# Placing the second batch's key maxima and value sums on VectorE: behind the weight conversions instead of among them

## The chip, the cores and the metric

One core of a Trainium2 chip runs the whole program. The metric is the device time of one execution in microseconds. TensorE (PE) does the matrix products, VectorE (DVE), ScalarE (ACT) and GpSimd (POOL) the work around them, SyncE (SP) starts the transfers. The order of the instructions on each engine's queue is fixed when the program is built.

## The reference, cut to what matters

Three layers follow each other on 2 x 768 tokens of width 512; the weights arrive as 8-byte floats.

```
k_sum = k.reshape(B, H, nb, 32, D).max(axis=3)      # 24 blocks of 32 keys: maximum of each
v_sum = v.reshape(B, H, nb, 32, D).mean(axis=3)     # and the mean of each block's values
scores = [q k^T / 8 inside a window of 15 on each side | q k_sum^T / 8 + log 32]
x = softmax(scores) @ [v | v_sum]                   # 8 heads, 2 batches
xk, xr = token mixes of x with the token before
y = sigmoid(xr w_r) * (relu(xk w_k)^2 w_v)          # "first layer": w_k 512x1024, w_v 1024x512
u = y + token mixing (w_tok1, w_tok2);  out = u + relu(u w_ch1) w_ch2
```

The change touches only when `k_sum` and `v_sum` of the second batch are computed on DVE.

## The kernel before, in words

**Weights.** The matmuls of the layers take each float32 operand as two parts, a rounded high part and a remainder; three products make one. A weight arrives as 128 x 512 eight-byte numbers and goes through `Weights.step` (L142 to L170): ACT scales the upper words (L153), DVE shifts the lower words (L157), DVE joins both to a float32 tile `wf` (L163), ACT rounds it to the high part (L174), POOL subtracts for the low part (L175, called from `rounded`, L172). `wf` has two buffers (WF = 2), so the shift of weight n + 2 needs the subtraction of weight n done. The first layer has 16 such weights: `wk[0], wv[0], wk[1], ... wv[7]`, in this order (L244 to L247).

**Attention.** Batch 0 runs as 12 steps of one half of the heads and one tile of 128 tokens, batch 1 as 6 steps of a whole tile. A step is: score matmuls (`sp`, L367), the masked and negated scores with their row extremes on DVE (L385), the exponential on ACT (L387), for batch 1 a normalization on DVE and POOL (`n_stage`, L394), transposes on PE (`pt`, L405), and the products with the values (`pv`, L425). Each key tile `kw` carries 24 columns of block maxima on either side; they are written there by POOL (`kw_sums`, L293) from the tile `ks`, which DVE's maxima fill (`k_max`, L287: one instruction for each of the six key tiles). All score matmuls of a batch thus need all six maxima of that batch. The value means: DVE sums (`vt_sum`, L309, two instructions into `vrs`), PE transposes (`v_gather`, L318), ACT scales into `vs` (L320), and SP copies `vs` into each value tile (L339) ahead of the value products.

**First layer.** `main` (L590) goes through six chunks of 256 tokens. For a chunk, `mixed` (L523) makes the mixed input (POOL L533, DVE L534, ACT L535, DVE L536). Then four groups: matmuls `ko` with two `wk` weights (24 instructions, one PSUM buffer), `k2_tile` (ACT relu L556, DVE square L557, ACT L558, POOL L559), and `values`, which adds the products with two `wv` weights into `acc` (12 instructions). Group 3 of the first chunk needs the 13th and 15th weight for `ko`, the 14th and 16th for `acc`. Chunks 0 to 2 need only batch 0; chunk 3 needs the first two tiles of batch 1.

**What sets the order.** The loop at L674 writes attention and first layer alternately by estimated costs; that order is each instruction's priority, which `ahead(n)` raises (k2_tile by 300, the transposes and value products by 400). A planner then simulates the engines and puts on each engine's queue what is ready, by priority. Before the first batch-1 score step, `prep(1)` (L512) writes the six `k_max`, the two `vt_sum`, `kw_sums` and `v_gather`. Walking through the two generators with their costs, all 16 weight conversions of the first layer have been written before the first `k_max` of batch 1, but the planner is free to place the maxima and the sums wherever DVE is free and their data has arrived. `behind(inst, marks)` (L227) is a pure ordering in a queue: `inst` is placed after the marked instruction, without a semaphore. Batch 0's `vt_sum` already has such a mark (`lows`).

Of the kernel before, what the change touches and what calls it, by code (L numbers as in the profile page):

```python
# [14 lines left out]
ALU = mybir.AluOpType  # L15
AX = mybir.AxisListType
# [41 lines left out]
def fused_kernel(ctx, tc, q, k, v, vt, mu, w_k, w_v, w_r, w_t1, w_t2, w_c1, w_c2, out):  # L58
    nc = tc.nc
# [40 lines left out]
    class Slot:  # L100


        def __init__(self, pl, tag):
            self.pl, self.tag = pl, tag
# [16 lines left out]
    class Weights:  # L121


        def __init__(self):
            self.todo, self.loaded, self.rounded, self.pin, self.ahead = [], [], [], 0, AHEAD
            self.early = True

        def add(self, slot, src, use):
            self.todo.append((slot, src, use))
# [12 lines left out]
        def step(self):  # L142
            while len(self.loaded) < self.ahead and self.todo:
                self.load()
            if not self.loaded:
                return False
            slot, st, use = self.loaded.pop(0)
            fold = isinstance(use, Fold)
            wf = use.part() if fold else stage.tile([128, 512], F32, tag="wf", bufs=WF, name="wf")
            words = st.bitcast(I32).rearrange("p (n two) -> p n two", two=2)  # L150
            top = words[:, :, 1]

            a = nc.scalar.activation(top.bitcast(F32), top.bitcast(F32), AF.Prelu, scale=2.0 ** -112, alpha=2.0 ** 32)  # L153
            after(a)
            behind(a, self.rounded[-2:-1])
            wi = wf.bitcast(I32)
            d = nc.vector.tensor_scalar(wi, words[:, :, 0], 29, None, ALU.logical_shift_right)  # L157
            after(d)
            if self.pin & 1:
                tc.keep_in_program_order(a)  # L160
            if self.pin & 2:
                tc.keep_in_program_order(d)
            nc.vector.scalar_tensor_tensor(wi, top, 3, wi, ALU.logical_shift_left, ALU.bitwise_or)  # L163
            if fold:
                use.close(slot)
            else:
                pair = slot.split("w")
                self.rounded.append(rounded(pair, wf, nc.gpsimd))
                use(pair)
            return True  # L170

    def rounded(pair, src, eng):  # L172
        hi, lo = pair
        r = nc.scalar.copy(hi, src)  # L174
        eng.tensor_tensor(lo, src, hi.bitcast(F32), ALU.subtract)  # L175
        return r
# [50 lines left out]
    def behind(inst, marks):  # L227

        for m in marks:
            tc.add_manual_dep(inst.ins, m.ins.name,  # L230
                              mybir.DependencyInfo(mybir.DependencyClass.NoSync, mybir.DependencyReason.DATA), reason="queue order")

    def after(inst):

        behind(inst, mark[-1:])

    weights = Weights()
# [17 lines left out]
    def ahead(n):  # L255

        def wrap(fn):
            def run(*args, **kw):
                with tc.high_priority(n) if n else ExitStack():
                    return fn(*args, **kw)  # L260
            return run
        return wrap

    state = {}
    lows = []
# [16 lines left out]
    def k_max(b, t):  # L282

        st = state[b]
        keys = st["kw"][t][:, :, K0 + PAD:K0 + PAD + 128].rearrange("p a (n w) -> p a n w", w=BLOCK)
        n = 128 // BLOCK
        nc.vector.tensor_reduce(st["ks"][:, :, n * t:n * t + n], keys, AX.X, ALU.max)  # L287

    @ahead(HK)
    def kw_sums(b, t):  # L290
# [13 lines left out]
    @ahead(HR)  # L304
    def vt_sum(b, j):
        st = state[b]
        if j == 0:
            st["vr"] = at.tile([128, NP, NB], F32, tag="vrs", bufs=1, name="vrs")
        r = nc.vector.tensor_reduce(st["vr"][:, 2 * j:2 * j + 2], st.pop(("vt", j)), AX.X, ALU.add)  # L309
        if b == 0:  # L310
            behind(r, lows[-1:])

    @ahead(HR)
    def v_gather(b):
# [134 lines left out]
    def attention():  # L449
# [3 lines left out]
        for i in range(len(steps) + 1):  # L453
            if i < len(steps):
                b, t, es = steps[i]
                if b and t == 0:
                    yield from prep(b)
                zs = s_stage(b, t, es)
                if len(es) == 1:
                    for what, z, lag in zip((t_stage, v_stage), (zs[0], zs), LAGS):  # L460
                        slots.setdefault(min(i + lag, n0), []).append(((i + lag, lag), what, z))
                else:
                    slots[i + 1] = [((i, 1), n_stage, z) for z in zs] + [((i, 2), t_stage, z) for z in zs] + [((i, 3), v_stage, zs)]
                if i < SPIN_UNITS:
                    spin(SPIN)
                yield 0.95 * len(es)
                if es[-1] == 1 and t + 1 < NT:
                    kw_sums(b, t + 1)
                if b and t == 0:
                    vw_sums(b, 0)  # L470
                if i in VSUM:
                    vt_sum(0, VSUM.index(i))
                if i == VSUM[1]:
                    v_gather(0)
                    vw_sums(0, 0)
# [36 lines left out]
    def prep(b):  # L512

        for t in range(NT):
            k_max(b, t)
            yield HOLD / (NT + 2)
        for j in range(2):
            vt_sum(b, j)
            yield HOLD / (NT + 2)
        kw_sums(b, 0)  # L520
        v_gather(b)
# [124 lines left out]
    for kind in range(3):  # L646
        mc = at.tile([128, NC], F32, name=f"mask{kind}")
        mm = work.tile([128, 2, 128], F32, tag="t32", bufs=2, name="mm")
        for half in range(2):
# [3 lines left out]
            keys = m[:, NB:NC] if half == 0 else m[:, 0:NK]  # L653
# [10 lines left out]
    for t in range(NT):  # L664
        ahead(HK)(k_max)(0, t)
# [477 lines left out]
```

## Time and profile before

| | |
|---|---|
| time, median of 3 runs | 502.85 us (502.44 to 504.47) |
| span of the profiled execution | 502.8 us, 8800 instructions |
| PE busy | 487.9 us, 97% of the span |
| DVE busy | 316.6 us, 63% |
| ACT busy | 250.9 us, 50% |
| POOL busy | 217.4 us, 43% |
| chain that ended last | PE 75%, DMA 10%, DVE 8%, POOL 2%, ACT 2% |
| granted PE clock, mean | 0.990 |

The profiled execution took 502.8 us from its first to its last instruction, 0.05 us from the median of the runs. In the page's second part the span is cut into 40 slices of 12.6 us; the PE line reads 9 nearly throughout, with 7 in slices 5 and 7 (counted from 1), the DVE line reads 9, 8, 9, 9 and 8 in slices 3 to 7 (25 to 88 us), and the clock line falls to 8 in slices 7 and 8. Busy PE is not PE at full speed: a matmul record that waits or runs at a lower clock is only longer.

### The profile page before, as it was taken

How to read it: one execution, taken by the hardware profiler on the slowest of the kernel's cores; microseconds unless marked ns; L12 is line 12 of the kernel's file. 1: busy time of each engine (PE TensorE's matmuls, PEld its weight loads, DVE VectorE, ACT ScalarE, POOL GpSimd, SP SyncE). 2: the span in 40 equal slices, each digit the busy share in tenths (PEclk: the TensorE clock that was granted, in tenths of full speed). 3: DMA queues.
4: the chain of work that ended last, by engine and by line, in shares of the span. 5: the costliest groups of instructions: out<-in, count | busy, mean ns of one | idle time of the engine just before them, and what ended most of it. 6: DMA issues, size and time to landing. Idle time of an engine off the chain costs nothing.

```text
span 502.8 us, 8800 instructions
## 1 busy us (share of the span) xinstructions
PE 487.9 (97%) x3278; PEld 407.1 (81%) x3278; DVE 316.6 (63%) x638; ACT 250.9 (50%) x569; POOL 217.4 (43%) x266
## 2 busy tenths in 40 slices
PE   7999997999999999999999998999999999999996
PEld 3567785888888888888888887878898999989995
DVE  2888998641514355598889789646579638354352
ACT  1778746862544555686585455454554435111110
POOL 6335587862441447345516434774942813000000
PEclk9899998899999999999999999999999999999999
DMA  8999930221000650000551998639351405253102
GB/s 264 323 309 361 335 87 14 88 80 40 20 1 2 224 196 0 1 0 14 161 163 21 400 394 313 211 112 316 117 168 42 142 31 164 52 200 117 52 1 83
DMA packets 35914, 70.63 MB, mean 140 GB/s; under 512 B 3072, under 2 KB 12288, under 8 KB 35872
## 3 DMA queue, kind: packets, MB, share of 16 engines
q1 hardware_dynamic: 34288, 69.09, 42.0%
q10 hardware_dynamic: 1584, 0.98, 0.7%
q8 instruction: 26, 0.43, 0.3%
q14 instruction: 16, 0.13, 0.1%
HBM read 60.04 MB, written 9.44 MB: 138 GB/s over the span
## 4 chain that ended last, share of the span: by engine, by line
PE 75%; DMA 10%; DVE 8%; POOL 2%; ACT 2%; issue 1%; SPq 1%; DVEq 0%; POOLq 0%
PE ko L544 13%; PE acc L544 13%; PE o L955 12%; PE m L544 11%; PE o L983 7%; PE ro L544 7%; PE go L544 5%; DMA wst<-in_moe_w_k_dram 3%; DMA xT<-in_q_dram 3%; DMA ybuf<-in_v_dram 2%; DVE wf L163 2%; PE pv L425 2%; PE sp L367 2%; PE h L544 2%; DMA wst<-in_moe_w_ch_dram 1%
## 5 line engine op out<-in xcount | busy, mean ns | idle before, releaser
L175 POOL TENSOR_TENSOR w<-wf,w 128x512 fp32r<-128x512 f32 x50 | 69.1, 1387 | 77.3 <-ACT w L174 72.4
L544 PE MATMUL ko<-xh,w 128*128 128x256 f32 x384 | 76.3, 288 | 1.7 <-POOL w L175 0.9
L544 PE MATMUL m<-u,w 128*128 128x256 f32 x504 | 65.1, 283 | 0.8 <-DVE mw L846 0.7
L544 PEld LDWEIGHTS m<-u,w 128*128 128x128 f32 x504 | 63.4, 191 | 2.9 <-DVE mw L846 0.9
L544 PEld LDWEIGHTS ko<-xh,w 128*128 128x128 f32 x384 | 61.1, 188 | 5.4 <-POOL w L175 1.1
L544 PE MATMUL acc<-w,kh 128*128 128x512 f32 x192 | 61.7, 404 | 0.0
L955 PE MATMUL o<-w,gh 128*128 128x512 f32 x192 | 59.1, 391 | 0.0
L544 PE MATMUL ko<-xl,w 128*128 128x256 f32 x192 | 54.4, 283 | 1.1 <-DVE xl L536 1.1
L559 POOL TENSOR_TENSOR kl<-rl,kh 128x512 fp32r<-128x512 f32 x24 | 33.7, 1405 | 44.6 <-ACT kh L558 36.4
L163 DVE SCALAR_TENSOR_TENSOR wf<-wst,wf 128x512 int32<-128x512 int32 x50 | 47.6, 956 | 8.2 <-ACT wst L153 7.1
L174 ACT CAST w<-wf 128x512 fp32r<-128x512 f32 x50 | 30.9, 620 | 42.8 <-DVE wf L163 40.9
L557 DVE TENSOR_TENSOR rl<-rl 128x512 f32<-128x512 f32 x24 | 19.6, 819 | 48.4 <-ACT rl L556 48.2
L387 ACT ACTIVATE pe<-pe,mn 128x120 f32<-128x120 f32 x96 | 36.6, 383 | 14.6 <-DVE mn L385 14.3
L153 ACT ACTIVATE wst<-wst 128x512 f32<-128x512 f32 x62 | 41.1, 675 | 2.1 <-DMA wst<-in_moe_w_ch_dram 2.1
L544 PEld LDWEIGHTS acc<-w,kh 128*128 128x128 f32 x192 | 35.3, 192 | 7.3 <-ACT pe L387 0.3
L955 PEld LDWEIGHTS o<-w,gh 128*128 128x128 f32 x192 | 34.7, 188 | 6.2
L534 DVE SCALAR_TENSOR_TENSOR xk<-xT,mus,tmp 128x256 f32<-128x256 f32 x52 | 36.5, 733 | 4.1 <-POOL tmp L533 3.2
L544 PEld LDWEIGHTS ko<-xl,w 128*128 128x128 f32 x192 | 36.2, 188 | 2.1 <-DVE xl L536 1.3
L544 PE MATMUL acc<-w,kl 128*128 128x512 f32 x96 | 37.7, 403 | 0.0
L955 PE MATMUL o<-w,gl 128*128 128x512 f32 x96 | 37.1, 391 | 0.0
L544 PE MATMUL go<-u,w 128*128 128x512 f32 x144 | 35.6, 393 | 0.0
L784 ACT ACTIVATE gh<-m 128x512 fp32r<-128x512 f32 x24 | 14.2, 596 | 42.7 <-DVE m L846 42.7
(120 smaller groups left out, 964.5 us busy)
## 6 DMA issues: line engine op xcount, KB each, us to landing
wst<-in_moe_w_ch_dram SPq DMA_DIRECT2D x36, 512.0 KB, 6.9
w<-stored SPq DMA_DIRECT2D x24, 512.0 KB, 4.9
stored<-w SPq DMA_DIRECT2D x24, 256.0 KB, 4.7
wst<-in_moe_w_k_dram SPq DMA_DIRECT2D x8, 512.0 KB, 7.4
wst<-in_moe_w_v_dram SPq DMA_DIRECT2D x8, 512.0 KB, 9.5
wst<-in_moe_w_tok_dram SPq DMA_DIRECT2D x6, 512.0 KB, 4.7
out_dram<-o SPq DMA_DIRECT2D x12, 256.0 KB, 2.4
kw<-in_k_dram SPq DMA_DIRECT2D x9, 320.0 KB, 5.1
```

What stands on the lines that cost most here:

```text
L153: a = nc.scalar.activation(top.bitcast(F32), top.bitcast(F32), AF.Prelu, scale=2.0 ** -112, alpha=2.0 ** 32)
L163: nc.vector.scalar_tensor_tensor(wi, top, 3, wi, ALU.logical_shift_left, ALU.bitwise_or)
L174: r = nc.scalar.copy(hi, src)
L175: eng.tensor_tensor(lo, src, hi.bitcast(F32), ALU.subtract)
L387: nc.scalar.activation(pe, pe, AF.Exp, bias=mn[:, p:p + 1], scale=-1.0, accum_out=den[:, p:p + 1])
L534: nc.vector.scalar_tensor_tensor(xk[:, d], xT[:, d, x0:x0 + MW], mu[:, d:d + 1], tmp, ALU.mult, ALU.add)
L544: nc.tensor.matmul(o, l, r, start=(first and i == 0), stop=(last and i == 3 * n - 1))
L557: nc.vector.tensor_tensor(rl, rl, rl, ALU.mult)
L559: nc.gpsimd.tensor_tensor(lo, rl, hi.bitcast(F32), ALU.subtract)
L784: nc.scalar.activation(hi, o, AF.Relu)
L955: nc.tensor.matmul(accs[c][t], l, r, start=(first and j == 0 and i == 0), stop=(last and j == 1 and i == 2))
L983: nc.tensor.matmul(accs[0][t], l, r, start=(k == 0 and i == 0), stop=(k == NF2 - 1 and i == 2))
```

## The change

The joined tile's instruction of each weight (L163) is remembered in a list. The maxima of batch 1 and the sums over its values are ordered on DVE's queue behind the last one in that list when they are written, which is the 16th weight, `wv[7]`. Batch 0's instructions keep their order. No arithmetic, no transfer and no buffer is added or taken away.

```
+            self.joined = []
...
-            nc.vector.scalar_tensor_tensor(wi, top, 3, wi, ALU.logical_shift_left, ALU.bitwise_or)
+            self.joined.append(nc.vector.scalar_tensor_tensor(wi, top, 3, wi, ALU.logical_shift_left, ALU.bitwise_or))
...
-        nc.vector.tensor_reduce(st["ks"][:, :, n * t:n * t + n], keys, AX.X, ALU.max)
+        r = nc.vector.tensor_reduce(st["ks"][:, :, n * t:n * t + n], keys, AX.X, ALU.max)
+        if b:
+            behind(r, weights.joined[-1:])
...
-        if b == 0:
-            behind(r, lows[-1:])
+        behind(r, weights.joined[-1:] if b else lows[-1:])
```

## Rows read from the trace of the kernel before

**Rows 1.** Stages: length, busy us of PE, PEld, DVE, ACT, POOL; PE clock; DMA.

```profile
55.00:75.00 20.00, 19.94 (x202) 16.61 (x203) 20.00 (x29) 9.35 (x16) 15.90 (x23) 1.00 0.62 181
75.00:80.00 5.00, 4.58 (x33) 3.50 (x28) 3.34 (x6) 3.09 (x6) 3.15 (x4) 1.00 0.00 0
80.00:85.00 5.00, 2.23 (x14) 1.82 (x14) 5.00 (x18) 2.99 (x8) 4.63 (x5) 0.89 0.00 0
85.00:90.00 5.00, 5.00 (x38) 3.48 (x37) 4.82 (x21) 3.86 (x17) 2.40 (x5) 0.50 0.28 73
90.00:95.00 5.00, 5.00 (x53) 3.93 (x53) 2.65 (x22) 3.85 (x19) 5.00 (x10) 0.92 0.40 127
95.00:300.00 205.00, 204.94 (x1375) 173.98 (x1374) 123.47 (x229) 120.91 (x255) 94.38 (x101) 1.00 0.31 103
```

**Rows 2.** PE's waits, 40 to 130 us: total us, times, longest.

```profile
PE sp L367 <- issue: 1.5, 1, 1.5
...
PE ko L544 <- POOL w L175: 0.9, 1, 0.9
PE ko L544 <- ACT rl L556: 0.7, 1, 0.7
```

**Rows 3.** Groups by line, DVE, 56.5 to 89 us: busy us, mean ns.

```profile
L163 DVE SCALAR_TENSOR_TENSOR wf<-wst,wf 128x512 int32<-128x512 int32 x8 | 7.7, 958 | 0.1
...
L157 DVE TENSOR_SCALAR wf<-wst 128x512 int32<-128x512 int32 x8 | 5.4, 671 | 1.2 <-POOL w L175 1.2
L287 DVE TENSOR_REDUCE ks<-kw 128x16 f32<-128x512 f32 x6 | 3.9, 668 | 0.0
L309 DVE TENSOR_REDUCE vrs<-ybuf 128x48 f32<-128x1536 f32 x2 | 3.5, 1740 | 0.0
```

**Rows 4.** DVE in order of time: start, length, instruction, idle before.

```profile
56.59 0.67 DVE L287 TENSOR_REDUCE ks<-kw 128x16 f32<-128x512 f32 x1
...
71.69 1.74 DVE L309 TENSOR_REDUCE vrs<-ybuf 128x48 f32<-128x1536 f32 x1
...
76.26 1.51 DVE L157 TENSOR_SCALAR wf<-wst 128x512 int32<-128x512 int32 x1 [1.18 <-POOL w L175]
...
79.08 0.42 DVE L157 TENSOR_SCALAR wf<-wst 128x512 int32<-128x512 int32 x1
...
83.73 0.27 DVE L385 CUSTOM_DVE_ANT_0 pe<-sp,mask 128x120 f32<-128x120 f32 x1
...
88.19 0.69 DVE L163 SCALAR_TENSOR_TENSOR wf<-wst,wf 128x512 int32<-128x512 int32 x1
```

**Rows 5.** Who waited for whom, all engines, 50 to 95 us.

```profile
ACT w L174 <- DVE wf L163: 7.2, 4, 3.0
POOL w L175 <- ACT w L174: 6.0, 2, 4.0
```

**Rows 6.** Groups by line, 55 to 90 us, POOL.

```profile
L175 POOL TENSOR_TENSOR w<-wf,w 128x512 fp32r<-128x512 f32 x8 | 11.2, 1403 | 2.0 <-ACT w L174 2.0
...
L533 POOL TENSOR_SCALAR tmp<-xT,oms 128x256 f32<-128x256 f32 x8 | 5.7, 713 | 4.5 <-DVE xT L445 4.1 <-DVE xk L534 0.4
...
L559 POOL TENSOR_TENSOR kl<-rl,kh 128x512 fp32r<-128x512 f32 x3 | 3.8, 1276 | 2.0 <-ACT kh L558 2.0
```

**Rows 7.** SP's queue: the copies of `vs` for batch 1.

```profile
83.97 4.38 SPq L339 DMA_DIRECT2D vw<-vs  x5
```

**Rows 8.** DVE later: input of chunk 3, its rounding, scores of batch 1's fifth step.

```profile
111.09 0.69 DVE L534 SCALAR_TENSOR_TENSOR xk<-xT,mus,tmp 128x256 f32<-128x256 f32 x1 [2.06 <-POOL tmp L533]
...
129.01 1.23 DVE L536 TENSOR_TENSOR xl<-xk,xh 128x1024 fp32r<-128x1024 f32 x1 [0.24 <-ACT xh L535]
...
136.94 0.28 DVE L385 CUSTOM_DVE_ANT_0 pe<-sp,mask 128x120 f32<-128x120 f32 x1 [1.68 <-PE sp L367]
```

**Rows 9.** The chain of waits: one group of `ko`, one of `acc`, at full clock.

```profile
130.71 3.04 PE ko L544 x24
133.75 2.80 PE acc L544 x12
```

## The prediction

> **What bounds the kernel now.** I read first the busy time by stage. From 95 to 300 us PE is busy 204.94 of 205 us at full clock, so what happens there can change the time only by adding or removing PE work, and the change does neither. [...] The idle part is 0.42 + 2.77 = 3.2 us. The clock part, busy time by the missing share of the clock, is 2.23 x 0.11 + 5.00 x 0.50 + 5.00 x 0.08 = 3.15 us. Together 6.3 us, the most that this stretch can give back. In the stretch before, 55 to 75 us, PE is idle for only 0.06 us, but DVE is busy 20.00 of 20 us [rows 1].
>
> PE's waits name the idle part: 1.5 us ahead of a score matmul, 0.9 us for a weight's low part from POOL, 0.7 us for the relu of `ko` [rows 2]; these add up to the 3.2. The middle one is the weight chain directly. The first is labelled "issue", so the profile names no releaser; by the code the second step's scores need the PSUM bank that DVE's first four score instructions of the first step release, and these began only at 83.73 [rows 4]. I take that for the releaser; it is an inference.
>
> Then I asked what kept DVE. By line it spent 7.7 us on joining eight weights, 5.4 on the shifts, and 3.9 + 3.5 = 7.4 us on batch 1's six maxima and two sums [rows 3]. In order of time the maxima begin at 56.59 and the second sum at 71.69, all among the conversions of weights 9 to 16; the join of the 16th starts at 88.19 and ends at 88.9 [rows 4]. So 7.4 us of work that the first layer's weights do not need stands ahead of them on an engine without a gap.
>
> **The change part by part.** *The 16th conversion.* The eight reductions leave the stretch ahead of it. If DVE is the limit, it ends up to 7.4 us earlier, and the first step's eight scores go behind too (8 x 0.27 = 2.2 us). Bound from the other side: 0, if the chain through ACT and POOL sets the pace. For DVE speaks that ACT waited 7.2 us for the join and POOL 6.0 us for ACT, who passes that wait on [rows 5]; POOL's own work, 11.2 + 5.7 + 3.8 = 20.7 us for the eight weights, the mixing and the remainders, fills little more than half of 35 us [rows 6]. Against it stands that the buffers allow only two weights at a time, and one shift waited 1.18 us for POOL [rows 4]. I take 5.5 us, nearer to the upper end: 83.4 us instead of 88.9.
>
> One shift took 1.51 us where the next took 0.42 [rows 4], each beside POOL work of a different kind; the mean join is 0.96 us and the reductions' mean, 0.668, hides no such tail [rows 3]. [...]
>
> *PE.* With weights 13 to 16 some 5 us earlier, the 0.9 us goes. The 0.7 us for the relu stays. Of the 1.5 us at the score bank I count half: the same dependence exists after the change, later. If PE's idle time in the stretch shrinks from 3.2 to about 1.5 us, spread out, most of the clock loss goes too: I take 2.6 of 3.15. Sum: 0.9 + 0.75 + 2.6 = 4.25 us gained.
>
> *What is later.* The eight reductions now take 7.4 us on DVE behind 83.4, so batch 1's scores begin at about 91 to 92 instead of 83.73. What moves with them: POOL's `kw_sums`, `v_gather` with its PE transposes and ACT's scaling, and SP's five copies, 4.38 us of issue that now start at about 91.5 instead of 83.97 [rows 7], with the value and query loads behind them on SP's queue. No transfer stands ahead of the reductions: keys and values of batch 1 had landed when they ran before. Does PE miss batch 1? The mixing for chunk 3, the first that needs it, began at 111.09, its rounding was finished from 129.01 on: 15 to 18 us of slack against a delay of 8. And the fifth step's scores came only at 136.94, so batch 1 ran ahead of its turn and then waited [rows 8]. As cover PE has chunk 1 and chunk 2, four groups each of 3.04 + 2.80 us [rows 9], about 47 us. So the delay costs nothing at the end. If this cover is not placed ahead of the scores, it costs up to 7.4 us (the third case below).
>
> *DVE behind the 16th weight.* The squares of `k2_tile` may stand behind a reduction: at best no loss, at worst all eight in a row, 7.4 us. The squares carry a priority raised by 300, so one reduction is the natural wait, at most 1.74 us [rows 4]. I take 0.7.
>
> Sum: 502.8 - 4.25 + 0.7 = 499.25, say 499.2. The profiled execution's span, 502.8, stands 0.05 us under the median of the runs, so no correction.
>
> **The rivals.** *All of it comes back.* The relu wait and the bank wait vanish as well, no square is held up, the clock never drops: 502.8 - 6.3 = 496.5. For it: DVE is full from 55 to 75. Against: POOL and DVE still meet, and the relu wait has nothing to do with the change.
>
> *The weights do not come earlier.* The two buffers and the chain shift, join, round, subtract set the pace, and what the reductions filled were DVE's gaps in the plan; or shifts and joins, closer together, meet POOL more often: if half of the sixteen took 1.51 instead of 0.42 us [rows 4], 8 x 1.1 = 8.8 us would eat the 7.4 saved. Then PE's starvation stays where it is; the first scores, displaced by 8 us, take with them 1 us of PE work that filled it, and the waiting at the bank goes: about 502.3, between 500.5 and 504.5. For it: the shift that waited for POOL. [...] Against: ACT's 7.2 us behind the join. In this case there is no change that can be measured; a measurement of this kernel tells about 0.5% (2.5 us).
>
> *Slower: PE stands in front of batch 1's scores.* PE's queue is in a fixed order. If the planner believes that the weights and the reductions are done some microseconds earlier than they are, it puts batch 1's first score matmuls ahead of the `ko` and `acc` work that could cover the 7.4 us, and PE waits with that work behind it. The price: with half the reductions uncovered 3.7 us idle, and a clock at half for another 5 us, 2.5 us; less the gain of 3.6: 502.8 + 2.6 = 505.4; with none covered 7.4 + 2.5 - 3.6, 509. It decides from the point where less than about one group (3.04 + 2.80 us) stands between the last weight's first use and the scores. For it: the 1.5 us at the score bank is just such a wait, in the queue of before. Against: by emission order the scores of that step come after two `ko` groups of chunk 1 and `acc` of its first, so there is cover of the right priority.
>
> **How the numbers follow.** Chances: my forecast 0.39, everything back 0.13, weights no earlier 0.26, PE in front of the scores 0.22. Faster by over 0.5% (under 500.3) takes the first two, 0.52; within 0.5% the third, 0.26; slower the fourth, 0.22. The likeliest case's own range is 497.0 to 500.3. The range for all begins at 496.5, the most the stretch can give, and ends at 505.4, the half-covered case; beyond the upper end lies about half of the slower case, below the lower one little, and replanned details after 300 us may cost or give another microsecond in any case.
>
> **What would show it.** Right: in the changed kernel the join of the 16th weight starts at 82 to 85 us, the first maximum of batch 1 directly behind it, scores at 90 to 93; between 75 and 95 us PE is idle under 2 us and no 5 us show a clock near 0.50; 95 to 300 stays full. Wrong in its first step: the 16th join still starts after 86.5. Wrong in its second: weights early, but a PE wait of over 2 us ahead of a batch 1 score, or a square behind several reductions. Wrong in its third: chunk 3's rounding late, and PE idle between 110 and 135.

## The result, and the profile after

The changed kernel takes 506.78 us (median of 4 runs, 506.64 to 507.48), 1.0076 times the kernel before, 95% interval 1.0055 to 1.0096: slower by 0.6 to 1.0%, about 4 us. The forecast was 499.2. The profiled execution took 507.48 us and shows a span of 505.7, so 1.8 us lie around a span. That also corrects a reading in the prediction: a span of 502.8 belongs to an execution of some 504.5 us, not to the median. It shifts the start of the sum by 1.7 us and not its sign. Two readings of the page of before, ahead of the prediction, are off too: its PE line has the 7 in slices 1 and 7, and its DVE line reads 8, 8, 9, 9, 8 in slices 3 to 7. The argument rests on [rows 1] and not on them.

The stages of the changed kernel, columns as in [rows 1]:

```profile
55.00:75.00 20.00, 16.49 (x140) 13.58 (x140) 19.72 (x24) 11.36 (x20) 14.31 (x13) 1.00 0.53 158
75.00:80.00 5.00, 3.99 (x21) 2.86 (x21) 4.05 (x5) 2.31 (x4) 3.72 (x3) 1.00 0.00 0
80.00:85.00 5.00, 5.00 (x34) 4.59 (x34) 5.00 (x8) 1.84 (x3) 3.14 (x3) 1.00 0.00 0
85.00:90.00 5.00, 5.00 (x45) 4.27 (x45) 4.81 (x5) 0.76 (x2) 2.88 (x13) 1.00 0.00 0
90.00:95.00 5.00, 5.00 (x59) 3.70 (x51) 1.43 (x1) 2.04 (x4) 2.56 (x2) 1.00 0.15 36
95.00:300.00 205.00, 205.00 (x1407) 170.98 (x1407) 126.62 (x274) 124.48 (x282) 97.74 (x112) 1.00 0.31 106
```

Against [rows 1] two things are as forecast and one is new. From 75 to 95 us, the stretch of the prediction's idle and clock parts, PE is idle 1.01 us instead of 3.2, and the clock no longer falls (1.00 in all four windows): that stretch gives back 2.2 us of idle and the 3.15 us of clock, 5.3 of its 6.3. (The clock part is that of the profiled execution, whose mean clock was 0.990. Of 35 other executions of the kernel before, on the chip of the first four experiments, the nine with a mean clock of 0.997 or more took 501.8 to 503.8 us and the six at 0.990 took 504.3 to 505.1, so this part is not lost every time.) New is 55 to 75, where PE idles 3.5 us. And 95 to 300 is as full as before, which hides the rest, as will be seen.

PE's waits, 40 to 130 us, where [rows 2] stood before:

```profile
PE spin L625 <- ACT rl L558: 1.7, 1, 1.7
...
PE acc L546 <- ACT kh L560: 1.0, 1, 1.0
PE ko L546 <- ACT rl L558: 1.0, 1, 1.0
...
PE acc L546 <- POOL kl L561: 0.8, 1, 0.8
```

DVE by line, 56.5 to 89 us, and some of its instructions in order of time (as [rows 3] and [rows 4]):

```profile
L164 DVE SCALAR_TENSOR_TENSOR wf<-wst,wf 128x512 int32<-128x512 int32 x8 | 11.3, 1417 | 0.4
L158 DVE TENSOR_SCALAR wf<-wst 128x512 int32<-128x512 int32 x8 | 6.7, 831 | 0.0
L288 DVE TENSOR_REDUCE ks<-kw 128x16 f32<-128x512 f32 x6 | 3.6, 669 | 0.0
...
L312 DVE TENSOR_REDUCE vrs<-ybuf 128x48 f32<-128x1536 f32 x2 | 3.4, 1733 | 0.0
L536 DVE SCALAR_TENSOR_TENSOR xk<-xT,mus,tmp 128x256 f32<-128x256 f32 x4 | 3.2, 818 | 0.0
```

where the last of these groups, the mixing, read before

```profile
L534 DVE SCALAR_TENSOR_TENSOR xk<-xT,mus,tmp 128x256 f32<-128x256 f32 x8 | 6.2, 781 | 0.4 <-POOL tmp L533 0.4
```

and in order of time, after:

```profile
81.06 0.68 DVE L164 SCALAR_TENSOR_TENSOR wf<-wst,wf 128x512 int32<-128x512 int32 x1
81.66 1.86 DVE L288 TENSOR_REDUCE ks<-kw 128x16 f32<-128x512 f32 x3
...
102.87 0.28 DVE L387 CUSTOM_DVE_ANT_0 pe<-sp,mask 128x120 f32<-128x120 f32 x1 [0.86 <-PE sp L369]
```

The 16th join starts at 81.06 instead of 88.19 and the maxima stand directly behind it. The joins grew from 0.96 to 1.42 us each, the shifts from 0.67 to 0.83: 4.9 us of the 7.4 that left. That the 16th join still comes 7.1 us earlier has a second reason: four of the eight mixing instructions (those of chunk 2; 6.2 us became 3.2) and the first step's eight scores (1.7 us busy) left the stretch as well. The first scores of batch 1 reach DVE at 102.87, not at 91 to 92: PE begins that step's matmuls at 89.10 and does them in five pieces, the last from 102.19 on.

How far the first layer is shows where the lead went. ACT's copies of a finished chunk, start in us, before:

```profile
106.90 0.56 ACT L587 COPY ybuf<-acc 128x512 f32<-128x512 f32 x1
...
135.88 1.28 ACT L587 COPY ybuf<-acc 128x512 f32<-128x512 f32 x2
163.09 1.28 ACT L587 COPY ybuf<-acc 128x512 f32<-128x512 f32 x2
...
193.61 0.57 ACT L587 COPY ybuf<-acc 128x512 f32<-128x512 f32 x1
```

and after:

```profile
96.01 1.29 ACT L589 COPY ybuf<-acc 128x512 f32<-128x512 f32 x2 [1.18 <-PE acc L546]
129.27 0.56 ACT L589 COPY ybuf<-acc 128x512 f32<-128x512 f32 x1
...
161.12 0.59 ACT L589 COPY ybuf<-acc 128x512 f32<-128x512 f32 x1 [1.18 <-PE acc L546]
...
196.19 0.58 ACT L589 COPY ybuf<-acc 128x512 f32<-128x512 f32 x1
```

By the first copy of each, chunk 0 is done 10.9 us earlier, chunk 1 6.6, chunk 2 2.0; the last half of chunk 3, by which batch 1's attention is through in both kernels, comes 2.6 us later. It stays near that to the end (span +2.9). From 55 us to that copy both traces hold the same matmuls (scores 192, transposes 56, `acc` 195, `ko` 422 and 421). So 3.5 us are lost before 75 and 5.3 won before 95, and still the same matmuls end 2.6 us later: they cost 2.6 - 3.5 + 5.3 = 4.4 us more of PE's time, nearly all of it after 95, where PE is "busy" in every window.

### The profile page after: what moved, and what is told of

The parts are those of the page before. It is cut to its first block, busy times and chain, and to the rows that moved or that the text cites. A ratio compares the mean times of both kernels' runs of the same rounds, so it can differ in the third digit from the quotient of the medians.

```text
span 505.7 us, 8788 instructions
## 1 busy us (share of the span) xinstructions
PE 488.6 (97%) x3278; PEld 406.2 (80%) x3278; DVE 321.9 (64%) x638; ACT 251.0 (50%) x569; POOL 217.7 (43%) x266
## 4 chain that ended last, share of the span: by engine, by line
PE 80%; DVE 9%; DMA 5%; issue 2%; ACT 2%; POOL 0%; SPq 0%; DVEq 0%; POOLq 0%
PE acc L546 12%; PE o L957 12%; PE ko L546 12%; PE m L546 11%; PE ro L546 7%; PE o L985 6%; PE go L546 5%; PE sp L369 4%; DVE wf L164 3%; PE pv L427 2%; PE pt L407 2%; DVE wf L158 2%; PE h L546 2%; DMA ybuf<-in_vt_dram 2%; PE spin L625 2%
## 5 line engine op out<-in xcount | busy, mean ns | idle before, releaser
L176 POOL TENSOR_TENSOR w<-wf,w 128x512 fp32r<-128x512 f32 x50 | 69.6, 1396 | 82.3 <-ACT w L175 76.1
L164 DVE SCALAR_TENSOR_TENSOR wf<-wst,wf 128x512 int32<-128x512 int32 x50 | 51.3, 1030 | 8.4 <-ACT wst L154 6.6
L561 POOL TENSOR_TENSOR kl<-rl,kh 128x512 fp32r<-128x512 f32 x24 | 33.4, 1393 | 37.0 <-ACT kh L560 30.1
L559 DVE TENSOR_TENSOR rl<-rl 128x512 f32<-128x512 f32 x24 | 21.3, 887 | 33.2 <-ACT rl L558 33.0
L536 DVE SCALAR_TENSOR_TENSOR xk<-xT,mus,tmp 128x256 f32<-128x256 f32 x52 | 34.6, 700 | 2.5 <-ACT tmp L533 1.2
```

The costliest lines, as they stand in the source:

```text
L164: self.joined.append(nc.vector.scalar_tensor_tensor(wi, top, 3, wi, ALU.logical_shift_left, ALU.bitwise_or))
L536: nc.vector.scalar_tensor_tensor(xk[:, d], xT[:, d, x0:x0 + MW], mu[:, d:d + 1], tmp, ALU.mult, ALU.add)
L559: nc.vector.tensor_tensor(rl, rl, rl, ALU.mult)
L561: nc.gpsimd.tensor_tensor(lo, rl, hi.bitcast(F32), ALU.subtract)
```

## The experiments

The first four runs set two theories against each other: A, the scores come too late; B, the conversions are packed too closely. What they left led to P, that every uninterrupted piece of score matmuls on PE costs a price of its own, so that more pieces cost more; and to its rival Q, that holding transposes back is good in itself. Ratios are to the kernel before, run on the same chip in five rounds, with 95% intervals; three chips were used (the first four runs on one, the next four on another, the last four on a third), so two ratios from different chips are compared less surely than either interval says. "Planned pieces" are counted in the instruction order on PE's queue: runs of batch 1's score matmuls, and of all transposes, that are not interrupted by another kind. Before: 18 and 40; changed kernel: 29 and 51.

**Delay without freeing DVE.**

```
-        eng.tensor_tensor(lo, src, hi.bitcast(F32), ALU.subtract)
+        low_parts.append(eng.tensor_tensor(lo, src, hi.bitcast(F32), ALU.subtract))
...
+            if b:
+                behind(r, low_parts[15:16])     # r: POOL's copy in kw_sums
```

> The kernel before, with one edit: POOL's copies of batch 1's block maxima into the key tiles are ordered on POOL's queue behind the low part of the 16th weight. DVE's maxima and sums stay where the planner puts them, among the conversions. Theory A (late scores): the changed kernel loses because batch 1's score steps leave the stretch in which PE waits for weights and come later, among ko and acc, where they cut the work into small pieces. Then this kernel, which delays the scores and frees no DVE time, loses too: 505.5 to 509 us. Theory B (packed conversions): the loss is that the conversions, without reductions between them, meet POOL's subtractions and hold up the squares of the first layer between 60 and 75 us. Then this kernel packs nothing and stands at 501.5 to 504.

506.63 us, 1.0048 (1.0024 to 1.0072). In theory A's range, over B's. But part of the loss is plain waiting, which neither theory named: PE waits 2.7 us ahead of scores for POOL's copies and is busy 13.12 of 20 us from 75 to 95, where before had 16.81.

**No reductions at all.**

```
+        if b:                                   # k_max; likewise vt_sum
+            if t == 0:
+                nc.gpsimd.memset(st["ks"], 1.0)
+            return
```

> The kernel before without batch 1's six maxima and two sums: their tiles are filled once with ones by POOL, so batch 1's block columns and block means are not computed. DVE has 7.4 us less, and nothing holds the scores back. Theory A: scores stay early, the weights come earlier, the clock does not drop: 497 to 500.5 us. Theory B: the conversions are packed as in the changed kernel, squares wait as there, and the time is 503 to 506 although 7.4 us of DVE work is gone.

505.68 us, 1.0048 (1.0027 to 1.0069): in B's range, far from A's. A kernel with 7.4 us less work is slower. But its scores were early for the first step only (85.6 us, then 113.6 and 127.6, where before had 83.7, 89.2 and 94.3) and planned in 23 and 49 pieces, so A's "early" did not hold here. Nor did B's "packed as in the changed kernel": the joins took 1.11 us in the mean, not 1.42. And the granted clock was 0.77 from 60 to 75 us, which neither theory has. The run could not decide.

**Maxima only.**

```
-        behind(r, weights.joined[-1:] if b else lows[-1:])
+        if b == 0:
+            behind(r, lows[-1:])
```

> Half of the change: the six maxima behind the 16th join, the two sums where the planner puts them. The scores need all maxima, so they are late as in the changed kernel, and 3.5 of the 7.4 us stay among the conversions. Theory A: 505 to 508, like the changed kernel. Theory B: half of its packing, 503.5 to 505.

505.51 us, 1.0041 (1.0022 to 1.0060). In A's range, 0.5 us over B's: no verdict. Here too PE waits ahead of scores for POOL's copies, 1.4 us.

**The changed kernel with blocks.**

```
-            nc.tensor.transpose(pt[:NC, p], z["P"][p], ident)
+            m = nc.tensor.transpose(pt[:NC, p], z["P"][p], ident)
+            if z["u"][0] and p == 0:
+                behind(m, mark[-1:])            # mark: last score matmul of each step written so far
```

> The changed kernel, with batch 1's transposes of a step ordered on PE's queue behind the last score matmul written before them, so that scores and transposes do not alternate in ones and twos (planned pieces of batch 1's scores 18 instead of 29, of transposes 27 instead of 51). Theory A with the cutting as its price: 3 to 5 us come back, 502 to 504.5. Theory A with the lateness itself as the price, or theory B: 505.5 to 508.

502.15 us, 0.9961 (0.9944 to 0.9978). One ordering on PE turns the loss into a gain, with the reductions where the change puts them, the joins as long (1.42 us) and the first scores about as late (101.5 us). So neither the lateness nor the packing can be what costs most of these 5.8 us (1.0076 to 0.9961). This is the decisive run. Score and transpose matmuls on PE, 95 to 182 us: records, busy us, mean ns. Before, changed kernel, changed kernel with blocks:

```profile
L405 PE MATMUL pt<-ident,pe 128*120 128x128 f32 x44 | 8.1, 278 | 0.0
L367 PE MATMUL sp<-kw,qT 64*64 64x120 f32 x96 | 5.9, 279 | 0.1
```

```profile
L369 PE MATMUL sp<-kw,qT 64*64 64x120 f32 x174 | 13.0, 280 | 0.0
L407 PE MATMUL pt<-ident,pe 128*120 128x128 f32 x48 | 11.3, 290 | 0.0
```

```profile
L369 PE MATMUL sp<-kw,qT 64*64 64x120 f32 x174 | 9.2, 276 | 0.0
...
L407 PE MATMUL pt<-ident,pe 128*120 128x128 f32 x48 | 7.1, 280 | 0.0
```

The same 174 and 48 records take 24.3 us in the changed kernel and 16.3 with blocks; before, 96 and 44 took 14.0, since the other scores had run ahead of 95 us. (A group's mean hardly shows it, and the busy sums, 8.0 us apart, overstate it: records overlap those of other groups, so what counts is the step from start to start.) One place, in order of time, changed kernel:

```profile
134.43 0.32 PE L407 MATMUL pt<-ident,pe 128*120 128x128 f32 x1
134.68 0.42 PE L369 MATMUL sp<-kw,qT 64*64 64x120 f32 x2
135.03 0.32 PE L407 MATMUL pt<-ident,pe 128*120 128x128 f32 x1
```

and with blocks:

```profile
134.57 0.85 PE L369 MATMUL sp<-kw,qT 64*64 64x120 f32 x24
135.35 1.09 PE L407 MATMUL pt<-ident,pe 128*120 128x128 f32 x8
```

Two score records cut off take 0.35 us from start to start (134.68 to 135.03), 24 together 0.78, or 0.033 each. The pair so costs about 0.28 us more than two records of a long piece. Over the stretch from 95 us to the last copy of chunk 3, scores come in 26 pieces in the changed kernel, in 15 with blocks and in 11 before. What entering and leaving them takes beyond the usual step of each kind (0.033 us for a score, 0.117 for `ko`, 0.234 for `acc`, 0.11 for a transpose) adds up to 8.3, 3.8 and 3.1 us: about 0.3 a piece in each trace. Since the last copy of chunk 3 starts at 190.53 with blocks and its trace is 1.39 us ahead already at chunk 0 (and at 57 us, ahead of all that differs), blocks give 196.19 - 190.53 - 1.39 = 4.3 us between: as much as the 4.4 that were missing.

**The kernel before with blocks** (the same edit).

> The kernel before with the edit of the run before last but one alone: batch 1's transposes behind the last score matmul written before them. Theory P (pieces): what the changed kernel loses is the price of each change of kind on PE, in its trace a score matmul ahead of another kind takes 0.19 us instead of 0.03, and entering scores costs 0.08 to 0.14. The kernel before has few pieces to lose (planned 18 of scores, 40 of transposes; with the edit 17 and 32), so the edit is worth under 1 us here: 502 to 503.5 beside 503.0. Rival theory Q: holding the transposes back is good in itself, whatever the pieces: 498.5 to 500.5 here too, and the change is still a loss beside it.

502.81 us, 0.9970 (0.9946 to 0.9993). In microseconds this is within P's range and above Q's, but the kernel before took 504.25 on this chip: by the ratio the edit is worth 1.5 us, more than P's "under 1" and less than Q's 2.5 to 4.5. Nearer to P; a share of Q is not excluded. Blocks are worth 0.3% here and 1.15% (1.0076 to 0.9961) in the changed kernel. With blocks in both, 0.9970 and 0.9961 cannot be told apart: DVE's new order itself neither gains nor loses what these runs can measure.

**More pieces, late.**

```
+HS1 = 100                                       # 200 in the next run
...
+        return ahead(HS1 if b else HS)(score_step)(b, t, es)
```

> The changed kernel with the priority of batch 1's score steps raised by 100: they come a little earlier, planned in 51 pieces instead of 29, transposes in 49 instead of 51. Theory P: 22 pieces more at 0.25 us, 5.5 us: 510 to 513. Theory A (lateness): slightly better than the changed kernel, 504.5 to 506.5. Theory Q: 506 to 508.

529.64 us, 1.0510 (1.0464 to 1.0555). P has the sign; A and Q are out; the size, some 21.5 us over the changed kernel by the ratios, is four times what P said. The stages, 95 to 130 and 130 to 182 us, columns as in [rows 1], show half of the reason:

```profile
95.00:130.00 35.00, 35.00 (x251) 27.41 (x250) 12.69 (x53) 15.38 (x48) 13.79 (x22) 0.85 0.18 51
130.00:182.00 52.00, 52.00 (x368) 37.40 (x367) 13.84 (x68) 21.79 (x72) 18.03 (x34) 0.90 0.14 45
```

```profile
118.64 0.39 PE L549 MATMUL ko<-xh,w 128*128 128x256 f32 x1
118.96 0.41 PE L372 MATMUL sp<-kw,qT 64*64 64x120 f32 x2
119.31 0.39 PE L549 MATMUL ko<-xl,w 128*128 128x256 f32 x1
...
124.16 0.66 PE L372 MATMUL sp<-kw,qT 64*64 64x120 f32 x2
```

The scores' pairs alternate with single `ko` matmuls, 0.67 us for a pair and one `ko` where by the usual steps they need about 0.19 together, and the granted clock falls to 0.85 and 0.90 although PE is busy 87 of 87 us. The clock alone takes 35 x 0.15 + 52 x 0.10 = 10.5 us, which P had not counted.

**Pieces, early** (the same edit with 200, on the kernel before).

> The kernel before with the priority of batch 1's score steps raised by 200: scores as early as before or earlier, planned in 30 pieces instead of 18, transposes in 41 instead of 40; reductions among the conversions as before. Theory P: 12 pieces more at 0.25 us, of which some fall into waits: 504.5 to 507. Theory A: scores are early, no loss: 501.5 to 503.5. Theory Q: 502 to 503.5.

514.00 us, 1.0179 (1.0126 to 1.0233). Again P's sign and more than its size: DVE's reductions are where they were and the scores are early, yet 9 us are lost; the clock is 0.90 from 130 to 182, which is 5.2 of them.

**Behind the 12th join, with blocks.**

```
-            behind(r, weights.joined[-1:])
+            behind(r, weights.joined[11:12])
```

> Both edits, with batch 1's reductions behind the 12th join instead of the 16th, and its transposes behind the scores: scores start almost as early as in the kernel before, planned pieces 15 of scores and 35 of transposes. Theory P with a use for PE's waiting time: no more pieces than before and the conversions somewhat earlier: 499.5 to 502, about the changed kernel with blocks or better. Theory Q: 500 to 502 as well; it does not tell these two apart, it asks whether all 16 conversions must go ahead.

504.19 us, 1.0011 (0.9989 to 1.0032). A miss: no loss, but no gain either. Few pieces do not suffice; here a transpose waits 2.2 us for POOL's normalization.

**Behind the 14th join, with blocks** (`joined[13:14]`).

> The change with the 14th join in place of the 16th, and blocks: planned pieces 13 and 31, scores a little earlier than in the changed kernel. Theory P: like the changed kernel with blocks or a little better, 500.5 to 502.5; the kernel with the 12th and blocks was at 1.0011 of the kernel before, so a value over 503 would say that the place of the scores matters beyond the pieces.

501.33 us, 0.9969 (0.9947 to 0.9991). As expected, and no better than the 16th with blocks.

**No reductions, with blocks.**

> The kernel before without batch 1's maxima and sums (their tiles filled with ones, so its block columns and means are not computed), and with its transposes behind the scores written before them: planned pieces 14 of scores and 26 of transposes. It asks what the 7.4 us on DVE are worth once the pieces are held together. Theory P: the left-out kernel without blocks lost to its pieces (23 and 49); with blocks it gains on it by 3 to 5 us and stands at 498.5 to 502, under the kernel before. If the conversions' own packing (theory B) is a loss of its own, it stays at 503 to 505.

500.27 us, 0.9935 (0.9917 to 0.9953). Blocks take the left-out kernel from 1.0048 to 0.9935. Beyond what blocks alone give (0.9970), that is 0.35%, under 2 us, for leaving out DVE's 7.4 us altogether; the two intervals touch, and their outer ends allow 0.76%. It does not bound the idea behind the change for every order: in this trace the clock was 0.77 from 60 to 75 us, so the planner's order loses something there too.

**Delay, with blocks.**

> The kernel with POOL's copies behind the 16th low part, and with blocks: planned pieces 12 and 27; scores late, reductions among the conversions. Theory P: the lateness as such costs little once the pieces are few: 501.5 to 504, 3 to 5 us under the same kernel without blocks. If lateness has a price of its own: 505 to 507 as before.

503.56 us, 1.0000 (0.9969 to 1.0031), from 1.0048 without blocks. So the scores can be late without a loss that shows. But this pair does not separate the pieces from the waits: without blocks PE waited 2.7 us ahead of scores for POOL's copies, and with blocks this wait is gone too.

**Sums only, with blocks.**

```
-        r = nc.vector.tensor_reduce(st["ks"][:, :, n * t:n * t + n], keys, AX.X, ALU.max)
-        if b:
-            behind(r, weights.joined[-1:])
+        nc.vector.tensor_reduce(st["ks"][:, :, n * t:n * t + n], keys, AX.X, ALU.max)
```

> Half of the change, the two sums (3.5 us) behind the 16th join and the maxima where the planner puts them, with blocks: scores early as in the kernel before, planned pieces 15 and 28. Theory P: first steps' scores still fall into PE's waits and DVE has 3.5 us less ahead of the weights: 499.5 to 502, the best so far. If freeing DVE is worth nothing: 501.5 to 503.5, like the kernel before with blocks.

505.16 us, 1.0034 (1.0018 to 1.0049). A miss. PE's waits, 55 to 300 us, say where:

```profile
PE ko L546 <- POOL w L176: 3.8, 2, 2.5
PE sp L367 <- issue: 1.2, 2, 0.7
```

Scores 15 and transposes 28 pieces, but `ko` waits 3.8 us for weights and the clock is 0.83 from 75 to 95: the planner's new order starves PE as the kernel before did, and more. From 56.5 to 92 us DVE's shifts wait 4.8 us for POOL's subtractions, which free the weights' two buffers. Why POOL came later than before was not tried.

## Why the prediction was wrong

*The 16th conversion* (forecast 5.5 us earlier, measured 7.1) and its effect on *PE* from 75 to 95 us (forecast 4.25 us, measured 5.3) had the right sign and about the right size, and DVE, not the chain, set the pace: it is busy 19.72 of 20 us from 55 to 75. So the rival "the weights do not come earlier" is out. The size of the first is in part luck: longer conversions took back 4.9 of the 7.4 us, and four mixing instructions that the forecast had not moved gave 3.0. The sum of POOL's work, 20.7 us, left out the copies of `kw_sums`; by [rows 1] POOL was busy 26.1 of the 35 us from 55 to 90.

The step that failed is under *What is later*: "So the delay costs nothing at the end." The sum has nothing for it; the trace shows 4.4 us. Its reasons were true as far as they went: chunk 3 was not starved, and chunks 1 and 2 covered the delay, PE has no wait from 95 to 300 us that the profile lists. But cover was counted as time that PE has to fill, and not what filling costs. Before, three of batch 1's score steps came ahead of 95 us, in seven pieces; three of these held 88 of the 96 matmuls, two of them at full clock:

```profile
71.06 1.04 PE L367 MATMUL sp<-kw,qT 64*64 64x120 f32 x28
...
93.05 1.04 PE L367 MATMUL sp<-kw,qT 64*64 64x120 f32 x30
```

Eleven pieces were left for the time after 95. In the changed kernel the planner puts five and a half steps there, between `ko`, `acc` and transposes, in 26 pieces, and each piece is paid. It shows in no idle column, since PE's records follow each other without a gap (205.00 of 205 us busy), only with less overlap. Blocks, which join the pieces again and leave the reductions where they are, bring 4.3 us back.

The second, smaller failure is *DVE behind the 16th weight*, 0.7 us for delayed squares. One square did stand behind all eight reductions, as the prediction's second sign of being wrong has it:

```profile
88.54 0.67 DVE L559 TENSOR_TENSOR rl<-rl 128x512 f32<-128x512 f32 x1
```

ACT waited 5.67 us for it, but PE is busy 15.00 of 15 us from 80 to 95, so no wait of PE came of it. The squares that PE waited for were delayed ahead of the 16th weight: joins of 1.42 us hold DVE there, and before 75 us PE waits 1.7 us for a relu, which on ACT stands behind a copy that waits for a join, and 1.0 + 0.8 us for the parts of a square, 3.5 in all. So the trace's sum is 5.3 gained, 3.5 and 4.4 lost: 2.6 us slower where 4.25 gained and 0.7 lost were forecast. That shifts and joins might grow, up to 8.8 us, was in the rival; the trace has 4.9, and the join still came 7.1 us earlier. Six of the eight joins took 1.57 to 1.79 us, each beside a subtraction of POOL (L176), and the two that ran with POOL idle 0.68 and 0.69. With the shifts it is alike: three took 1.37 to 1.52 us beside a subtraction of POOL (L176 or L561), four that began with POOL idle 0.41 to 0.42. Why they are longer there no row shows. What part of the 3.5 us is due to the longer conversions and what to the queue's order was not separated. Taking reductions away cannot be the whole reason for the longer joins: with none at all (*No reductions at all*) they took 1.11 us.

The slower rival had the right outcome with the wrong place: it let PE stand idle ahead of batch 1's first scores, and in the changed kernel there is no such wait. What a change of kind costs on PE was not weighed, and that is the true cause. The scores run as 64 x 64 tiles, `ko` and `acc` as 128 x 128: two score records between transposes take 0.35 us where two among their kind take 0.066, while from `ko` to `acc`, both 128 x 128, the next start comes after 0.12 us as within `ko` (0.117). What TensorE does in the time between is in no row here.

The fastest kernels here that compute everything are the change with blocks, 0.9961, and the change behind the 14th join with blocks, 0.9969, but the kernel before with blocks, 0.9970, is their equal.

## What to carry to other kernels

Work moved to another place in a full engine's queue can cost more there, if it comes in more pieces (here 26 of scores against 15, 4.3 us). Before moving it, count in the instruction order how many uninterrupted pieces it will come in and price a piece from start to start. The count is no guarantee: two kernels here with 15 pieces of scores gained nothing; in their traces PE waited elsewhere. Then compare progress marks (a finished chunk) between two traces, not busy shares: a full PE can lose 4 us without an idle gap.

## What the runs showed of the hardware

Two score records of 64 x 64 tiles take 0.066 us among their kind and 0.35 between others. A stretch in which such pairs alternate with single 128 x 128 matmuls, 95 to 130 us, had PE busy 35.00 of 35 us and still a mean granted clock of 0.85; the changed kernel, with its longer runs, kept 1.00 there. And the joins, the same eight instructions, went from 0.96 to 1.42 us in the mean when only the order around them was changed: 1.57 to 1.79 beside a subtraction of POOL, 0.68 and 0.69 with POOL idle.
